# Strassen's seven products for the first matrix product of the 512-row expert tiles, and a moved half of that product

## The chip, the cores and the metric

The kernel runs on one core of a Trainium2 chip. A core has five engines that run side by side, each with its own queue of instructions taken in order: TensorE (PE, matrix products into the eight PSUM banks), VectorE (DVE), ScalarE (ACT), GpSimd (POOL, [...]which also issues the row scatters) and SyncE (SP, which issues the other DMA transfers). They wait for one another through semaphores. The metric is the device time of the one launch in microseconds (us), as the median of its timed runs.

## What is computed

The input is 8 batches of 2496 tokens of 256 channels. Each batch is filtered in the frequency domain along its tokens; then each token goes to one of 8 experts, which is a two-layer network with a ReLU between.

```python
X = np.fft.rfft(x, axis=1)
y = np.fft.irfft(X * (filt_r + 1j * filt_i)[None], n=2496, axis=1)     # (8, 2496, 256)
x = y.reshape(19968, 256)
logits = x @ w_gate                                                    # (19968, 8)
e = np.argmax(logits, axis=1)
gate = softmax(logits)[rows, e]
for each expert e, over its rows:  h = np.maximum(x[rows] @ w1[e], 0)  # w1[e]: 256 x 1024
                                   out[rows] = gate * (h @ w2[e])      # w2[e]: 1024 x 256
```

All of it is in fp32.

## The kernel before

**Transforms.** The Fourier transforms are matrix products, done batch by batch in four stages: `stage_a` (L331), `stage_b` (L344, with the filter as four VectorE instructions, L358 to L362), `stage_c` (L365) and `stage_d` (L381). Between stages the data goes to DRAM and back. The loads share a pool of input tiles (`NIN` = 8 of them, L295) and the finished rows wait in `YB` = 8 tiles until they are scattered.

**Routing.** `route` (L498) finds each token's expert on VectorE and computes a row number in a DRAM list kept by expert (`row`, L576). GpSimd scatters the rows there, one indirect DMA for each group of rows (L596). `tile_map` then cuts the lists into tiles that all hold rows of one expert: 28 tiles of 512 rows, 14 of 256 and at the end 23 of 128.

**Experts.** A tile is worked in steps. `rows_in` and `weights` issue the loads of its rows (`xg`) and of the halves of its weights: `w1t` in two halves of 512 hidden channels, `w2t` likewise, each in three buffers. `turn_x` (L716) transposes the rows on TensorE into `xT` (two blocks of 128 channels). `hidden` (L729) makes 128 hidden channels by all rows of the tile: two matmuls (L733) into one PSUM bank, and a ReLU out of it (L737) into one of nine `hT` tiles; eight such steps make the first product. `result` (L740) makes 128 output rows: eight matmuls (L747) into a bank, the gate on ScalarE or VectorE (L751, L752) into one of four `ys` tiles, and a row scatter on GpSimd (L753).

**Order.** The order on TensorE, VectorE, ScalarE and SyncE is that in which the program emits the steps. A planner (the loop from L912) does this with a clock of its own: `experts` (L875) yields expert steps with costs and with the load that each needs, the transform steps come from `STEPS`, and the planner takes an expert step when its load is due and the expert work has credit, else a transform step. Routing steps go in between. `prefetch` (L860) issues loads as buffers come free in this plan. GpSimd's order is left to the scheduler of the language. For a tile i, `experts` yields `turn_x(i)` unless it was done, eight `hidden` steps, `turn_x(i + 1)` if its rows are due, and then the `result` steps:

```python
for k in range(FT):
    yield lambda: hidden(i, k), 0.43 * n, ("w1", 2 * i + k // FH2)
...
for j in range(n):
    yield lambda: result(i, j), 3.42, ("w2", 2 * i + 1)
```

The transforms end at some 1033 us; from there on only expert tiles are left, first ten of 512 rows.

Of the kernel before, what the change touches and what calls it, by code (L numbers as in the profile page):

```python
# [22 lines left out]
E = 8  # L23
# [95 lines left out]
def kernel(  # L119
# [77 lines left out]
    tau_i = cst.tile([1, 64], I32, name="tau_i")  # L197
# [3 lines left out]
    pro = first.enter_context(tc.tile_pool(name="pro", bufs=2, side="right"))  # L201
    pools = {}
# [92 lines left out]
    NIN, YB = 8, 8  # L295
# [48 lines left out]
    def stage_b(b, f):  # L344
# [10 lines left out]
        yw = sb.tile([P, 2, D], F32, tag="yw", name="yw")  # L355
# [258 lines left out]
    def tile_map(b, rows, n, last):  # L614
# [21 lines left out]
        tau = pools["moe"].tile([1, n], F32, tag=f"tau{n}", name="tau", bufs=1)  # L636
        past = pools["moe"].tile([1, n, E - 1], F32, tag=f"past{n}", name="past", bufs=1)
# [5 lines left out]
        ef = pools["moe"].tile([1, n], F32, tag=f"ef{n}", name="ef", bufs=1)  # L643
# [5 lines left out]
        rf = pools["moe"].tile([1, n], F32, tag=f"rf{n}", name="rf", bufs=1)  # L649
# [24 lines left out]
    work, idt, gts, xgs, xts, w1t, w2t, hs = [], {}, {}, {}, {}, {}, {}, {}  # L674
# [22 lines left out]
    def weights(h, second):  # L697
# [10 lines left out]
        if second:  # L708
            w2t[h] = pools["moe"].tile([P, FH2, D], F32, tag="w2t", name="w2t", bufs=3)
            nc.sync.dma_start(out=w2t[h], in_=moe_w2[bass.ds(ev, 1), k].rearrange("o p i d -> p (o i) d"))  # L710
        else:
            pool, bufs = (late["w1"], 8) if i >= SHORT else (pools["moe"], 3)
            w1t[h] = pool.tile([P, DH, F // 2], F32, tag="w1t", name="w1t", bufs=bufs)
            nc.sync.dma_start(out=w1t[h], in_=moe_w1[bass.ds(ev, 1), k].rearrange("o p i f -> p (o i) f"))

    def turn_x(i):  # L716
# [5 lines left out]
        xts[i] = pools["moe"].tile([P, DH, 4 * P], F32, tag="xT", name="xT", bufs=1)  # L722
        for dh in range(DH):
# [3 lines left out]
            evac(xts[i][:, dh, :n * P].rearrange("p (j q) -> p j q", j=n), pt[:, :n], n * P)  # L727

    def hidden(i, k):  # L729
        m = work[i][0] * P  # L730
        p = bank()
        for dh in range(DH):
            mm(p[:, :m], lhsT=w1t[2 * i + k // FH2][:, dh, k % FH2 * P:(k % FH2 + 1) * P], rhs=xts[i][:, dh, :m],  # L733
               start=(dh == 0), stop=(dh == DH - 1))
        hT = pools["moe"].tile([P, 512], F32, tag="hT", name="hT", bufs=9)
        either(m, lambda: nc.vector.tensor_scalar_max(hT[:, :m], p[:, :m], 0.0),
               lambda: nc.scalar.activation(hT[:, :m], p[:, :m], AF.Relu))  # L737
        hs.setdefault(i, []).append(hT)

    def result(i, j):  # L740
# [4 lines left out]
        for k in range(FT):  # L745
            w2 = late["w2s"][:, bass.ds(ev, 1), k, :] if i >= SHORT else w2t[2 * i + k // FH2][:, k % FH2, :]
            mm(p[:, :D], lhsT=hs[i][k][:, j * P:(j + 1) * P], rhs=w2, start=(k == 0), stop=(k == FT - 1))  # L747
        ys = pools["moe"].tile([P, D], F32, tag="ys", name="ys", bufs=4)
# [111 lines left out]
    def prefetch():  # L860
# [6 lines left out]
        for what in ("w1", "w2"):  # L867
            h = got[what]
            if h < 2 * len(work) and rows_at[work[h // 2][3]] <= now[0] and (
                    h - used[what] < (3 if h < 2 * SHORT else 8)):  # L870
# [4 lines left out]
    def experts():  # L875

        for i in range(NT):
            n = TILES[i][0]
            if used["x"] == i:
                yield lambda: turn_x(i), 0.22 * n, ("x", i)  # L880
                used["x"] += 1
            for k in range(FT):
                yield lambda: hidden(i, k), 0.43 * n, ("w1", 2 * i + k // FH2)
                if (k + 1) % FH2 == 0:
                    w1t.pop(used["w1"])
                    used["w1"] += 1
            xts.pop(i)
            if i + 1 < NT and when.get(("x", i + 1), now[0] + 1.0) <= now[0]:
                yield lambda: turn_x(i + 1), 0.22 * TILES[i + 1][0], ("x", i + 1)
                used["x"] += 1  # L890
            for j in range(n):
# [4 lines left out]
    def share():  # L896

        known = sum(7.1 * t[0] for t in work[used["w2"] // 2:])
# [71 lines left out]
```

## Time and profile before

| | |
|---|---|
| timed runs | 1622.03 us median of 3 (1621.72 to 1622.7) |
| profiled execution, span | 1618.2 us, mean granted TensorE clock 0.989 |
| TensorE, first product of the 512-row tiles (L733) | 896 records of 128x512 |
| TensorE, second product with `w2t` (L747) | 2240 records of 128x256, 502.1 us |
| VectorE, ScalarE, GpSimd busy in 1033 to 1331 us (512-row tiles alone) | 18.59, 73.31, 47.00 us of 298 |
| data moved | 287.36 MB, 178 GB/s in the mean |

The profile is of one execution. Busy time is the time in which an engine had an instruction at work. The chain is followed back from the last instruction, at each step to what released it or to the instruction before it on its engine. A wait is put down to the instruction that ended last before it. A group is written as line, engine, operation, output tile <- input tiles, shapes and count, then busy us and mean ns of one, and then the idle time of the engine before these instructions and what ended it. An fp32 matmul appears as two records, an fp32 transpose as one.

### The profile page before, as it was taken

To read this page: it belongs to the slowest core of one execution; us is meant where nothing else is said; L and a number is where in the kernel's file an instruction comes from. 1 tells how busy PE (TensorE), PEld (TensorE's weight loads), DVE (VectorE), ACT (ScalarE), POOL (GpSimd) and SP (SyncE) were. 2 spreads that over 40 slices of the span, in tenths; PEclk is the share of its full clock that TensorE was granted. 3 is DMA by queue.
4 is the path that set the end of the run, shared out by engine and by line. 5 is a ranking of instruction groups with operands and counts; after the bars stand their busy time and mean duration, and the time that the engine had idled before them with its cause. 6 is when DMAs were issued, how large, how long until landed. Compare 5 with 4: busy or idle time off the path is not lost.

```text
span 1618.2 us, 21005 instructions
## 1 busy us (share of the span) xinstructions
PE 1567.2 (97%) x6760; PEld 1080.1 (67%) x6760; DVE 423.3 (26%) x1418; ACT 518.1 (32%) x1149; POOL 366.6 (23%) x379
## 2 busy tenths in 40 slices
PE   7989899999999999999999899999999999999998
PEld 6534456677566666666666567667676678899997
DVE  4576561624512422235222212300000000000000
ACT  4434343333322232323233232222222222333433
POOL 4132222304213221023113205411111111111111
PEclk9998999999999999999999999999999999999999
DMA  8669797887945584347434624433344446566551
GB/s 241 173 174 285 231 317 241 248 264 234 293 130 163 171 253 133 118 149 199 136 107 129 181 82 157 153 105 110 133 148 154 135 150 227 178 219 183 172 181 47
DMA packets 119265, 287.36 MB, mean 178 GB/s; under 512 B 17587, under 2 KB 58812, under 8 KB 119157
## 3 DMA queue, kind: packets, MB, share of 16 engines
q1 hardware_dynamic: 99941, 242.69, 49.8%
q0 software_dynamic: 19216, 43.33, 7.7%
q8 instruction: 55, 0.90, 0.2%
q14 instruction: 53, 0.43, 0.1%
HBM read 205.95 MB, written 80.90 MB: 177 GB/s over the span
## 4 chain that ended last, share of the span: by engine, by line
PE 89%; DMA 4%; DVE 3%; issue 2%; SPq 0%; ACT 0%; POOL 0%; POOLq 0%; ACTq 0%; DVEq 0%
PE bank L747 34%; PE bank L733 34%; PE bank L391 4%; PE bank L351 3%; PE bank L372 3%; PE bank L337 3%; PE bank L726 2%; PE bank L466 2%; DMA fin<-ud 1%; PE lt L480 1%; DMA ud<-uo 1%; DMA fin<-in_x_dram 1%; PE bank L413 1%; DMA zd<-zo 1%; DVE yw L360 1%
## 5 line engine op out<-in xcount | busy, mean ns | idle before, releaser
L733 PE MATMUL bank<-xT,w1t 128*128 128x512 f32 (+2 forms) x2080 | 589.2, 435 | 0.2 <-ACT xT L227 0.2
L747 PE MATMUL bank<-w2t,hT 128*128 128x256 f32 x2240 | 502.1, 381 | 0.3 <-issue 0.3
L733 PEld LDWEIGHTS bank<-xT,w1t 128*128 128x128 f32 x2080 | 337.7, 191 | 218.5 <-issue 196.4
L747 PEld LDWEIGHTS bank<-w2t,hT 128*128 128x128 f32 x2240 | 422.9, 191 | 74.9 <-issue 18.4
L753 POOL DMA_INDIRECT out_dram<-ys,idt x163 | 160.1, 982 | 914.3 <-ACT ys L752 604.9
L737 ACT ACTIVATE hT<-bank 128x512 f32<-128x512 f32 (+2 forms) x520 | 227.4, 438 | 360.2 <-PE bank L733 325.0
L596 POOL DMA_INDIRECT rows<-yo,row x176 | 174.8, 993 | 299.1 <-DVE gts L721 69.0
L752 ACT ACTIVATE ys<-bank,gts 128x256 f32<-128x256 f32 x157 | 74.2, 474 | 493.4 <-PE bank L747 450.6
L227 DVE COPY xT<-bank 128x128 f32<-128x128 f32 (+2 forms) x53 | 25.1, 473 | 583.3 <-PE bank L726 467.8
L372 PE MATMUL bank<-ys,tcs 128*128 128x512 f32 x140 | 74.3, 613 | 13.6 <-DVE ys L362 10.2
L358 DVE TENSOR_TENSOR ys<-bank,ht 128x512 f32<-128x512 f32 x80 | 55.1, 689 | 122.5 <-PE bank L351 83.9
L747 PE MATMUL bank<-w2s,hT 128*128 x368 | 83.2, 379 | 0.0
L391 PE MATMUL bank<-fin,tds 120*117 120x512 f32 x140 | 69.8, 622 | 12.1 <-DMA fin<-ud 12.1
L337 PE MATMUL bank<-fin,tas 117*120 117x512 f32 x154 | 73.9, 598 | 0.0
L747 PEld LDWEIGHTS bank<-w2s,hT 128*128 128x128 f32 x368 | 68.1, 190 | 8.3
L351 PE MATMUL bank<-fin,tbs 128*128 128x512 f32 x140 | 72.4, 600 | 0.0
L227 ACT COPY uo<-bank 128x512 f32<-128x512 f32 x70 | 41.0, 586 | 70.1 <-PE bank L372 51.9
L359 DVE SCALAR_TENSOR_TENSOR yw<-bank,ht 64x512 f32<-64x512 f32 x80 | 55.4, 693 | 2.6 <-POOL ht L253 1.2
L360 DVE TENSOR_TENSOR yw<-bank,ht 64x512 f32<-64x512 f32 x80 | 54.7, 684 | 1.1
L391 PEld LDWEIGHTS bank<-fin,tds 120*117 120x117 f32 x140 | 25.8, 188 | 43.4 <-issue 31.6
L227 ACT COPY yo<-bank 117x512 f32<-117x512 f32 x70 | 40.6, 589 | 41.3 <-PE bank L391 34.8
L372 PEld LDWEIGHTS bank<-ys,tcs 128*128 128x128 f32 x140 | 25.9, 193 | 39.5 <-issue 28.8
(129 smaller groups left out, 885.0 us busy)
## 6 DMA issues: line engine op xcount, KB each, us to landing
w1t<-in_moe_w_dram SPq DMA_DIRECT2D x130, 512.0 KB
w2t<-in_moe_w_dram SPq DMA_DIRECT2D x84, 512.0 KB
fin<-in_x_dram SPq DMA_DIRECT2D x40, 512.0 KB
fin<-zd SPq DMA_DIRECT2D x70, 256.0 KB
ud<-uo SPq DMA_DIRECT2D x70, 256.0 KB
zd<-zo SPq DMA_DIRECT2D x35, 480.0 KB
fin<-ud SPq DMA_DIRECT2D x35, 480.0 KB
xg<-rows SPq DMA_DIRECT2D x28, 544.0 KB
```

The costliest lines, as they stand in the source:

```text
L227: either(n, lambda: nc.vector.tensor_copy(o, i), lambda: nc.scalar.copy(out=o, in_=i))
L337: mm(p[:TK, :], lhsT=tas, rhs=xt[:TP, j:j + 2, :], start=True, stop=True)
L351: mm(p, lhsT=tbs, rhs=zi[:, j:j + 2, :], start=True, stop=True)
L360: nc.vector.tensor_mul(yw[HP:], z2[:HP], fi)
L372: mm(p, lhsT=tcs, rhs=ys, start=True, stop=True)
L391: mm(p[:TP, :], lhsT=tds, rhs=ui[:TK, j:j + 2, :], start=True, stop=True)
L596: sc = nc.gpsimd.indirect_dma_start(out=rowsd, out_offset=bass.IndirectOffsetOnAxis(ap=at, axis=0), in_=what, in_offset=None,)
L733: mm(p[:, :m], lhsT=w1t[2 * i + k // FH2][:, dh, k % FH2 * P:(k % FH2 + 1) * P], rhs=xts[i][:, dh, :m], start=(dh == 0), stop=(dh == DH - 1))
L737: lambda: nc.scalar.activation(hT[:, :m], p[:, :m], AF.Relu))
L747: mm(p[:, :D], lhsT=hs[i][k][:, j * P:(j + 1) * P], rhs=w2, start=(k == 0), stop=(k == FT - 1))
L752: lambda: nc.scalar.activation(ys, p[:, :D], AF.Copy, scale=gate))
L753: nc.gpsimd.indirect_dma_start(out=out, out_offset=bass.IndirectOffsetOnAxis(ap=idt[i].bitcast(U32)[:, j, :], axis=0), in_=ys, in_offset=None,
```

## The change

The first product of a 512-row tile is done by Strassen's method, in the form with fifteen additions. For each half of the hidden channels the weights `w1t` are seen as 2x2 blocks (128 input channels x 256 hidden channels) and the tile as 2x2 blocks (128 channels x 256 rows). Seven products of blocks (`product`, two matmuls of 256 columns each into one bank) take the place of eight. The weight sums (`w1_sums`, four additions for a half) and the row sums (four additions for a tile, at the end of `turn_x`) are made on GpSimd. The products are put together by seven VectorE additions out of PSUM and one ScalarE copy, through a tile `part` and in `hT`; two ReLUs of 1024 columns on ScalarE then work in place. Tiles of 256 and 128 rows keep the plain product.

`experts` now yields the first product by halves, and puts the first half of the next tile's first product ahead of a tile's `result` steps when its rows and weights are due by the plan. The weight sums of the next half are issued in the middle of a half, when its weights are due.

To make room, `NIN` goes from 8 to 7, `YB` from 8 to 6, `w2t` from three buffers to two, `ys` from four to three, the routing scratch tiles share buffers and two small tiles move to other pools; `xT` goes from one buffer to two, and `hT` is three tiles of half a product each. The host lays `w1` out so that a half holds two blocks of 256 channels; a load has the size it had.

```diff
-    NIN, YB = 8, 8
+    NIN, YB = 7, 6
...
-        yw = sb.tile([P, 2, D], F32, tag="yw", name="yw")
+        yw = (pro if b == 0 else sb).tile([P, 2, D], F32, tag="yw", name="yw", bufs=2 if b == 0 else 1)
...
-            w2t[h] = pools["moe"].tile([P, FH2, D], F32, tag="w2t", name="w2t", bufs=3)
+            w2t[h] = pools["moe"].tile([P, FH2, D], F32, tag="w2t", name="w2t", bufs=2)
...
-        xts[i] = pools["moe"].tile([P, DH, 4 * P], F32, tag="xT", name="xT", bufs=1)
+        xts[i] = pools["moe"].tile([P, DH, 4 * P], F32, tag="xT", name="xT", bufs=2)
...
+        if n == 4:
+            b = xts[i].rearrange("p h (r c) -> p h r c", r=2)
+            t = sums[i] = pools["moe"].tile([P, 4, 2 * P], F32, tag="sums", name="sums", bufs=2)
+            nc.gpsimd.tensor_tensor(t[:, 0], b[:, 0, 1], b[:, 0, 0], op=ALU.subtract)
+            nc.gpsimd.tensor_tensor(t[:, 1], b[:, 1, 1], t[:, 0], op=ALU.subtract)
+            nc.gpsimd.tensor_tensor(t[:, 2], b[:, 1, 1], b[:, 0, 1], op=ALU.subtract)
+            nc.gpsimd.tensor_tensor(t[:, 3], b[:, 1, 0], t[:, 1], op=ALU.subtract)
+            free["p"] = max(free["p"], now[0]) + 3.0
+
+    def w1_sums(h):
+        w = w1t[h]
+        t = wsum[h] = pools["moe"].tile([P, 4, 2 * P], F32, tag="wsum", name="wsum", bufs=2)
+        nc.gpsimd.tensor_tensor(t[:, 0], w[:, 0, 1], w[:, 1, 1], op=ALU.add)
+        nc.gpsimd.tensor_tensor(t[:, 1], t[:, 0], w[:, 0, 0], op=ALU.subtract)
+        nc.gpsimd.tensor_tensor(t[:, 2], w[:, 0, 0], w[:, 0, 1], op=ALU.subtract)
+        nc.gpsimd.tensor_tensor(t[:, 3], w[:, 1, 0], t[:, 1], op=ALU.subtract)
+        free["p"] = max(free["p"], now[0]) + 3.0
+
+    def hidden_by_quarters(h):
...
+        def product(left, right):
+            q = bank().rearrange("p (v c) -> p v c", v=2)
+            for v in range(2):
+                mm(q[:, v], lhsT=left[:, v * P:(v + 1) * P], rhs=right, start=True, stop=True)
+            return q
...
+        low = hT[:, 1, :, 0]
+        q = product(w[:, 0, 0], b[:, 0, 0])
+        nc.scalar.copy(out=part, in_=q)
+        q = product(w[:, 1, 0], b[:, 1, 0])
+        add(hT[:, 0, :, 0], q, part)
+        yield 1.71
+        q = product(ws[:, 1], t[:, 1])
+        add(part, q, part)
+        q = product(ws[:, 2], t[:, 2])
+        add(low, q, part)
+        yield 1.71
+        q = product(ws[:, 0], t[:, 0])
+        add(hT[:, 1, :, 1], q, low)
+        add(part, q, part)
+        q = product(w[:, 1, 1], t[:, 3])
+        add(low, q, low)
+        relu(hT[:, 1], hT[:, 1])
+        yield 1.71
+        q = product(ws[:, 3], b[:, 1, 1])
+        add(hT[:, 0, :, 1], q, part)
+        relu(hT[:, 0], hT[:, 0])
+        yield 0.85
...
-        ys = pools["moe"].tile([P, D], F32, tag="ys", name="ys", bufs=4)
+        ys = pools["moe"].tile([P, D], F32, tag="ys", name="ys", bufs=3)
...
+        def half(h):
+            i, g = divmod(h, 2)
+            n = TILES[i][0]
+            if n == 4:
+                if h not in wsum:
+                    yield lambda: w1_sums(h), 0.0, ("w1", h)
+                steps = hidden_by_quarters(h)
+                for m, t in enumerate((1.71, 1.71, 1.71, 0.85)):
+                    yield lambda: next(steps), t, ("w1", h)
+                    if m == 1 and due("w1", h + 1) and TILES[(h + 1) // 2][0] == 4:
+                        w1_sums(h + 1)
+                wsum.pop(h)
+            else:
+                for a in range(4):
+                    yield lambda: hidden(i, g, a), 0.43 * n, ("w1", h)
...
         for i in range(NT):
-            n = TILES[i][0]
-            if used["x"] == i:
-                yield lambda: turn_x(i), 0.22 * n, ("x", i)
-                used["x"] += 1
-            for k in range(FT):
-                yield lambda: hidden(i, k), 0.43 * n, ("w1", 2 * i + k // FH2)
...
-            if i + 1 < NT and when.get(("x", i + 1), now[0] + 1.0) <= now[0]:
-                yield lambda: turn_x(i + 1), 0.22 * TILES[i + 1][0], ("x", i + 1)
-                used["x"] += 1
-            for j in range(n):
+            yield from turned(i)
+            if used["w1"] == 2 * i:
+                yield from half(2 * i)
+            if due("x", i + 1):
+                yield from turned(i + 1)
+            yield from half(2 * i + 1)
+            if used["x"] == i + 2 and due("w1", 2 * i + 2):
+                yield from half(2 * i + 2)
+            for j in range(TILES[i][0]):
                 yield lambda: result(i, j), 3.42, ("w2", 2 * i + 1)
...
-        known = sum(7.1 * t[0] for t in work[used["w2"] // 2:])
+        known = sum(26.8 if t[0] == 4 else 7.1 * t[0] for t in work[used["w2"] // 2:])
```

## The prediction

> **What bounds the kernel now.** I read the page's busy times first, then the chain that ended last, then the granted clock and the busy times by stretch, then the groups by shape for prices.
>
> ```profile
> PE 1567.2 (97%) x6760; PEld 1080.1 (67%) x6760; DVE 423.3 (26%) x1418; ACT 518.1 (32%) x1149; POOL 366.6 (23%) x379
> PE 89%; DMA 4%; DVE 3%; issue 2%; SPq 0%; ACT 0%; POOL 0%; POOLq 0%; ACTq 0%; DVEq 0%
> ```
>
> The second line is the chain by engine. TensorE is busy 97% of the span and carries 89% of the chain, so work taken from TensorE shortens the kernel, as long as nothing makes it wait. The same chain in order of time gives its prices, undisturbed, after the transforms have ended:
>
> ```profile
> 1161.72 13.73 PE bank L733 x32
> 1176.33 13.82 PE bank L747 x64
> ...
> 1331.82 6.91 PE bank L733 x32
> ```
>
> Columns: start, length, line, count. A matrix product in fp32 shows as two records. A 512-row tile's first product (L733) takes 13.73 us in 32 records of 512 columns, 0.429 us each. The 256-row tile after 1331 takes 6.91 us in 32 records of 256 columns, 0.216 us each, and changes its PSUM bank every four records, exactly as the new products do: narrower instructions cost the same per column.
>
> ```profile
> 130.00:165.00 35.00, 30.21 (x100) 14.04 (x98) 21.52 (x74) 16.15 (x33) 5.82 (x6) 0.90 0.99 287
> 1100.00:1200.00 100.00, 100.00 (x359) 65.86 (x358) 2.52 (x9) 25.36 (x46) 13.68 (x14) 1.00 0.39 132
> ```
>
> These are stretches: busy TensorE, weight loads, VectorE, ScalarE, GpSimd, then granted clock, DMA share, GB/s. Until about 240 us there is little expert work to fill with, the DMA engines are nearly full (0.99) and TensorE has gaps; later it has none. So a step may use any other engine late, but early there is no slack.
>
> ```profile
> L358 DVE TENSOR_TENSOR ys<-bank,ht 128x512 f32<-128x512 f32 x80 | 55.1, 689 | 122.5 <-PE bank L351 83.9 <-PE bank L747 11.4 <-issue 9.5
> L737 ACT ACTIVATE hT<-bank 128x512 f32<-128x512 f32 x224 | 133.8, 598 | 274.3 <-PE bank L733 247.7 <-issue 26.5
> L362 POOL TENSOR_TENSOR ys<-ys,yw 128x512 f32<-128x512 f32 x10 | 12.7, 1268 | 15.7 <-DVE yw L360 7.7 <-PE bank L351 3.3 <-PE bank L337 3.1
> L253 POOL TENSOR_TENSOR ht<-ht,sgs 64x1024 f32<-64x1024 f32 x4 | 7.6, 1892 | 15.0 <-DMA ht<-in_filt_dram 14.8
> L253 POOL TENSOR_TENSOR ht<-ht,sgs 64x512 f32<-64x512 f32 x2 | 2.1, 1035 | 0.1
> ```
>
> Prices: an add of a PSUM bank and an SBUF tile on VectorE is 0.69 us (L358 has these operands), a 512-wide ReLU on ScalarE 0.60 us. The 224 ReLUs are eight for each of 28 tiles of 512 rows. GpSimd adds are shown at 512 and 1024 elements only.
>
> **What the Trainium skill says.** "GPSIMD Engine Reference", section 3.1, measures an add of 2048 fp32 at 4497 ns. With the 1268 ns here at 512 this gives 2.1 ns an element and, as an estimate, 0.73 us at the 256 of the change; L253's two rows give 1.67 ns an element and 0.61 us. "SBUF — State Buffer", section "Who interferes with whom", says that a VectorE instruction with at most one SBUF input does not contend with GpSimd. All seven new VectorE adds have one input in PSUM, so I add nothing for contention; no run here shows it. "ScalarE: Activation LUTs", section "What ACT_TABLE_LOAD costs", gives 186 ns + 0.833 ns an element, 1.04 us for the new 1024-wide ReLU; at 512 it gives 0.61, and the trace 0.60.
>
> **The change, part by part.** *Products.* Half a tile's first product is four steps of two 512-column matmuls now, 6.87 us. It becomes seven products of two 256-column matmuls, 28 records x 0.216 = 6.05 us. 56 halves x 0.82 = **45.9 us** off TensorE. The built program has 784 such matmuls (56 x 14), so it does what it says.
>
> *Evacuation.* Per half, VectorE gets seven adds, 7 x 0.69 = 4.83 us, and ScalarE one copy and two ReLUs, 0.59 + 2 x 1.04 = 2.67 us in place of 4 x 0.60 = 2.40. Both are below TensorE's 6.05, so the seven banks hold; a half ends some 2 us after its last matmul (add 0.69, ReLU 1.04). Nothing waits for that: the next tile's half, 6.05 us, stands in between. This is what the moved step is worth, and I put both at 0. In the transform stage VectorE's adds come on top of 20 to 37% busy (400 to 1000 us) and make it about 50 to 70% with 9.7 us a tile; the transform's own additions (L358 to L362, 2.8 us in a row) may hold an add up, so 0 to 14 us (0.8 us for each of some 18 tiles); I take 0.
>
> *GpSimd sums.* Twelve adds a tile, 12 x 0.73 = 8.8 us, and four row writes at 1.29 us from start to start, 5.2 us: 14 us of a 27 us tile. In the late stage the order on TensorE is turn, half, half of the next tile, four results. The sums needed by the third product of the next tile's half (six adds deep) start about 2.2 us after the results end and are done at 2.2 + 4.4 = 6.6; they are needed at 0.9 + 6.05 + 1.73 = 8.7. So there is 2 us to spare, and the cost is 0.
>
> *The first 512-row tile* is different. In the program's order on GpSimd its sums stand around the row scatters of the second batch: sums, one scatter, one weight sum, three sums, three weight sums, seven scatters, four weight sums. The trace of before shows when that scatter can go:
>
> ```profile
> 241.00 1.04 PE L726 MATMUL bank<-ident,xg 128*128 128x128 f32 x8
> 241.65 1.07 ACT L227 COPY xT<-bank 128x512 f32<-128x512 f32 x2 [0.36 <-PE bank L726]
> 246.19 0.17 DVE L576 CAST row<-rowf 117x8 uint32<-117x8 f32 x1
> 246.66 1.00 POOL L596 DMA_INDIRECT rows<-yo,row  x1 [20.48 <-DVE gts L721]
> 247.96 0.99 POOL L596 DMA_INDIRECT rows<-yo,row  x1 [0.30 <-issue]
> ```
>
> GpSimd waits until 246.66 for the row numbers. The sum that the third product needs is the fifth add behind that scatter: 247.96 + 5 x 0.73 = 251.6. TensorE is ready at 242.29 + 1.73 = 244.0 and waits 7.6. Then it has five products (4.3), transposes (0.5) and two products (1.7) until 258.1, while GpSimd does two adds (253.1), seven scatters (9.0, 262.1) and three adds: 264.3. It waits 6.2. TensorE takes its instructions in order, so the transforms behind it wait as well. In sum **+13.7 us**; bounds 0 (if scatters and sums fell otherwise) and 20 (adds at 1.27 us). After these gaps the clock will dip, as in the stretch 130 to 165 (0.90): +1, between 0 and 3.
>
> *The end of the transforms.* The last batch has fourteen scatters in a row (18 us) besides the 14 us of that tile, against 27: some 5 us over, less the slack. I take **+2**, between 0 and 7.
>
> *Buffers.* One input tile fewer (`NIN` 7), `YB` 6: the queue order of SyncE has some loads one or two places later, behind stores that wait for ScalarE. Where DMA was the chain before 240 us this may cost a load's latency (about 5 us) or nothing; other places gain, since nearby products are reordered. **+2**, between -3 and +8. `w2t` with two buffers: both halves load only after the results before; 1 MB at the 152 GB/s of a late tile is 7 us, hidden by two halves (12.1 us). `ys` with three: a row is written every 3.45 us and needed again after 10.4; hidden. The further `yield` rules, the 256- and 128-row tiles and the routing scratch change no count of instructions: 0.
>
> *Sum:* -45.9 + 13.7 + 1 + 2 + 2 = -27.2 us on the profiled span of 1618.2, hence 1591. The three timed runs stand 3.8 us above that span, and I make no claim on this difference: 1622.0 - 27.2 = **1595 us**.
>
> **Rivals.** (A) *No wait at the first tile*, because the scatters do not hold the sums as the order says: only -45.9 and small terms, 1576 to 1584. For it: elsewhere the sums have 2 us or more to spare. Against: GpSimd takes its queue in order, and the trace shows it idle 20 us for that scatter. Chance 0.17. (B) *Small waits in each transform-stage tile*, VectorE's adds behind the transform's own: 18 x 0.8 = 14 us more, 1604 to 1618. For it: chains of four VectorE instructions before 240 us already set the end. Against: half of VectorE is still free. Chance 0.20. (C) *GpSimd becomes the bound:* the place is the third product of each moved half, the price six adds. It decides from (8.7 - 2.2) / 6 = 1.08 us an add; at 1.5 us each of 27 tiles waits 2.5 us, 68 us, with 20 at the first tile: 1622 - 46 + 68 + 20 + 5 = 1669, slower than before. For it: the trace shows no add of this size. Against: twice the width took 1.27. Chance 0.05. That losses just eat the gain: 0.03.
>
> **Numbers.** My own case, 1585 to 1603, gets 0.55. The range for 8 in 10 reaches into A and B, 1579 to 1611. A difference under 0.2%, 3.2 us, cannot be told from none here. Faster by more: 0.92; within: 0.03; slower: 0.05.
>
> **What would show it.** The new product's line at 12.1 us for 28 pairs of a tile, and a late tile of 26.8 us where it was 28.4; TensorE waiting for GpSimd twice, 6 to 8 us each, between 240 and 270 us, and hardly elsewhere; VectorE near 690 us busy, GpSimd near 610. I am wrong if TensorE waits for GpSimd or VectorE in every tile, or if the stage before 240 us lasts over 8 us longer.

## The result, and the profile after

The change makes the kernel faster, by a quarter of what was forecast.

| | before | after |
|---|---|---|
| time, median | 1622.28 us (4 runs) | 1615.65 us (4 runs, 1614.27 to 1618.16) |
| ratio, 95% interval | | 0.9961 [0.9944, 0.9978] |
| span of the profiled execution | 1618.2 us | 1612.5 us |

The forecast was 1595 us with a range from 1579 to 1611. The time lies above that range; the sign was right.

The page of the changed kernel, its busy times and its chain by engine:

```profile
PE 1536.1 (95%) x7432; PEld 1211.1 (75%) x7432; DVE 694.7 (43%) x1797; ACT 533.5 (33%) x1106; POOL 608.5 (38%) x715
PE 31%; issue 1%; DMA 0%; POOL 0%; POOLq 0%; ACT 0%
```

VectorE (694.7) and GpSimd (608.5) are busy for what was forecast (690 and 610). TensorE's busy time fell by 31.1 us, not by 45.9, and the chain, which TensorE carried to 89% before, can be followed on it for 31% only. Its first and some later pieces, in order of time (start, length, what, count):

```profile
1090.71 0.98 DMA out_dram<-ys,idt
1091.69 4.05 issue
...
1095.91 0.98 POOL out_dram L827
...
1096.91 0.75 POOL sums L733
...
1097.73 0.73 POOL sums L734
...
1119.18 12.09 PE bank L765 x56
1131.27 13.86 PE bank L821 x64
1145.13 0.87 PE bank L727 x8
1146.00 12.09 PE bank L765 x56
```

It begins with a row write of the results, waits 4 us, goes over the next row write and two sums on GpSimd, and only then runs on TensorE; I come back to that. From there on a tile's first product takes 12.09 us in 56 records, and one tile follows the next after 26.8 us, where it was 28.4. There the change brings all it can, and TensorE waits for nothing.

The loss is in two other stretches. Busy times by stretch of the changed kernel (columns as in the prediction: stretch, length, TensorE, weight loads, VectorE, ScalarE, GpSimd, then granted clock, DMA share, GB/s):

```profile
130.00:165.00 35.00, 29.11 (x104) 14.53 (x105) 20.09 (x70) 16.30 (x33) 5.84 (x6) 0.92 1.05 324
225.00:275.00 50.00, 38.85 (x156) 28.49 (x155) 27.36 (x99) 15.35 (x30) 16.29 (x20) 0.83 0.73 238
1000.00:1110.00 110.00, 97.78 (x448) 83.78 (x447) 48.99 (x134) 28.41 (x43) 65.68 (x80) 0.95 0.38 123
1100.00:1200.00 100.00, 100.00 (x477) 88.04 (x476) 46.55 (x121) 27.41 (x41) 46.14 (x60) 0.99 0.36 116
```

and the two stretches in the kernel before:

```profile
225.00:275.00 50.00, 47.10 (x202) 28.55 (x201) 18.36 (x85) 18.26 (x37) 11.87 (x12) 1.00 0.84 279
1000.00:1110.00 110.00, 109.65 (x410) 74.47 (x409) 17.55 (x104) 26.94 (x50) 34.38 (x36) 1.00 0.41 136
```

The reader is to see two things in each pair: TensorE is idle for 8 and 12 us more, and its granted clock is lower (0.83 and 0.95 for 1.00). The second is a loss that busy time hides, since a slow matmul counts as busy.

To have both in one number I took, in each trace, the time from the start of every TensorE record to the start of the next, less the median of that time for the records of its line and shape (those that signal a semaphore are counted apart from those that don't). The medians add up to the work at full speed, the rest is what was lost to waits and to half clock.

```
                          work    lost, us, in the stretch
                        (medians)  0-225  225-275  275-1000  1000-1110  1110-end   sum
kernel before            1523.5     49.7      4.9      28.1        0.8      -0.2   83.3
changed kernel           1477.3     47.0     19.8      40.1       17.1      -0.2  123.8
difference                -46.2     -2.7    +14.9     +12.0      +16.3       0.0  +40.5
```

-46.2 + 40.5 = -5.7 us is the difference of the two spans. So the products bring what was forecast, and 40 us of waits and half clock take most of it away: 15 at the first 512-row tile, 16 at the end of the transforms, 12 spread between them, less 3 ahead of them.

*The first 512-row tile*, TensorE in the changed kernel (start, length, line, what it does, count, and the wait before it):

```profile
238.62 0.66 PE L537 MATMUL rk<-oe,tri 117*117 117x64 f32 x2 [3.44 <-DVE oe L526]
...
241.23 3.66 PE L765 MATMUL bank<-xT,w1t 128*128 128x256 f32 x8
249.55 5.48 PE L765 MATMUL bank<-sums,wsum 128*128 128x256 f32 x12 [4.66 <-POOL wsum L744]
...
257.03 1.89 PE L765 MATMUL bank<-xT,w1t 128*128 128x256 f32 x8
261.98 4.39 PE L765 MATMUL bank<-sums,wsum 128*128 128x256 f32 x12 [3.06 <-POOL wsum L744]
...
267.94 1.24 PE L806 MATMUL bank<-xT,w1t 128*128 128x256 f32 x5
```

Eight records take 1.89 us at full clock (257.03) and 3.66 at half (241.23). The tile takes 267.94 - 241.23 = 26.7 us, where its products and transposes need 12.6. Of the 14.1 us lost, 7.7 are the two waits for GpSimd that the prediction named, and the other 6.4 are nearly all half clock (5.9 by the trace's record of the clock). Not all of it follows from these two waits: the first eight records are slow already. Ahead of them TensorE had waited 3.44 us for the routing (L537). In the kernel before that wait is 2.66 us long, and no half clock follows it.

*The end of the transforms.* GpSimd first, then ScalarE, then TensorE:

```profile
1080.31 0.73 POOL L746 TENSOR_TENSOR wsum<-w1t,wsum 128x256 f32<-128x256 f32 x1
1081.21 1.00 POOL L827 DMA_INDIRECT out_dram<-ys,idt  x1 [0.17 <-issue]
1087.53 0.99 POOL L827 DMA_INDIRECT out_dram<-ys,idt  x1 [5.32 <-ACT ys L826]
1090.71 0.98 POOL L827 DMA_INDIRECT out_dram<-ys,idt  x1 [2.20 <-issue]
1095.91 0.98 POOL L827 DMA_INDIRECT out_dram<-ys,idt  x1 [4.22 <-ACT part L778]
1096.91 0.74 POOL L733 TENSOR_TENSOR sums<-xT 128x256 f32<-128x256 f32 x1
```

```profile
1086.87 0.47 ACT L826 ACTIVATE ys<-bank,gts 128x256 f32<-128x256 f32 x1 [11.92 <-DMA out_dram<-ys,idt]
```

```profile
1087.39 2.07 PE L765 MATMUL bank<-sums,wsum 128*128 128x256 f32 x4 [5.82 <-ACT ys L826]
...
1098.51 4.26 PE L765 MATMUL bank<-sums,wsum 128*128 128x256 f32 x12 [4.69 <-POOL sums L734]
```

From 1058 to 1081 us GpSimd works without a pause on fourteen row scatters and eight weight sums. The four row writes of the results (L827) come behind them. ScalarE, with three result buffers, waits 11.9 us for the first of them to land before it can write the fourth result, and behind it in its queue stands the evacuation of TensorE's banks: TensorE waits 5.8 us. The sums of the next tile stand behind the four row writes: TensorE waits another 4.7. What is odd is how the row writes go: not one every 1.29 us as the scatters do, but over 14.7 us.

### The profile page after: what moved, and what is told of

It reads as the page before. It is cut to its first block, busy times and chain, and to the rows that moved or that the text cites. A ratio compares the mean times of both kernels' runs of the same rounds, so it can differ in the third digit from the quotient of the medians.

```text
span 1612.5 us, 23212 instructions
## 1 busy us (share of the span) xinstructions
PE 1536.1 (95%) x7432; PEld 1211.1 (75%) x7432; DVE 694.7 (43%) x1797; ACT 533.5 (33%) x1106; POOL 608.5 (38%) x715
## 5 line engine op out<-in xcount | busy, mean ns | idle before, releaser
L827 POOL DMA_INDIRECT out_dram<-ys,idt x163 | 160.8, 986 | 610.8 <-ACT ys L826 326.4
L596 POOL DMA_INDIRECT rows<-yo,row x176 | 175.0, 994 | 223.1 <-issue 54.5
L773 ACT ACTIVATE hT<-hT 128x1024 f32<-128x1024 f32 x112 | 113.7, 1052 | 292.9 <-DVE hT L769 253.2
L806 PE MATMUL bank<-xT,w1t 128*128 128x128 f32 (+1 forms) x1184 | 191.9, 317 | 0.3 <-issue 0.3
L765 PE MATMUL bank<-sums,wsum 128*128 128x256 f32 x672 | 165.9, 393 | 19.4 <-POOL wsum L744 7.7
L806 PEld LDWEIGHTS bank<-xT,w1t 128*128 128x128 f32 x1184 | 169.3, 193 | 20.0 <-issue 9.3
L765 PEld LDWEIGHTS bank<-sums,wsum 128*128 128x128 f32 x672 | 129.7, 197 | 50.4 <-issue 10.5
L769 DVE TENSOR_TENSOR hT<-bank,part 128x512 f32<-128x512 f32 x168 | 115.6, 688 | 117.5 <-ACT part L778 63.0
L812 ACT ACTIVATE hT<-bank 128x128 f32<-128x128 f32 (+1 forms) x295 | 93.4, 318 | 81.7 <-PE bank L806 68.2
L765 PE MATMUL bank<-xT,w1t 128*128 128x256 f32 x448 | 108.5, 386 | 0.4 <-ACT yo L227 0.4
L765 PEld LDWEIGHTS bank<-xT,w1t 128*128 128x128 f32 x448 | 83.7, 193 | 15.3 <-issue 3.3
L769 DVE TENSOR_TENSOR part<-bank,part 128x512 f32<-128x512 f32 x112 | 76.7, 685 | 18.0 <-PE bank L765 14.5
L769 DVE TENSOR_TENSOR hT<-bank,hT 128x512 f32<-128x512 f32 x112 | 76.8, 685 | 8.9 <-PE bank L765 4.2
L391 PE MATMUL bank<-fin,tds 120*117 120x512 f32 x140 | 69.6, 620 | 7.4 <-DMA fin<-ud 7.4
```

What stands on the lines that cost most here:

```text
L391: mm(p[:TP, :], lhsT=tds, rhs=ui[:TK, j:j + 2, :], start=True, stop=True)
L596: sc = nc.gpsimd.indirect_dma_start(out=rowsd, out_offset=bass.IndirectOffsetOnAxis(ap=at, axis=0), in_=what, in_offset=None,)
L765: mm(q[:, v], lhsT=left[:, v * P:(v + 1) * P], rhs=right, start=True, stop=True)
L769: nc.vector.tensor_tensor(o, q, a, op=ALU.add)
L773: nc.scalar.activation(o, q, AF.Relu)
L806: mm(p[:, :m], lhsT=w1t[2 * i + g][:, dh, fh, v * P:(v + 1) * P], rhs=xts[i][:, dh, :m], start=(dh == 0), stop=(dh == DH - 1))
```

## The experiments

Each ratio is against the kernel before, timed in the same set on the same chip. Ratios of different sets compare badly: the changed kernel as it is gave 0.9961 in the first set and 0.9916 in another. So what one edit does is read from the stretch that it concerns, in its trace. "Lost" is the number defined above.

### The parts of the change one by one

**Plain products, moved half kept.** `STR` is the set of tiles that use the seven products; here it is empty.

```diff
-        if n == 4:
+        if i in STR:
...
-            if n == 4:
+            if i in STR:
                 if h not in wsum:
```

> The changed kernel with the seven products taken out again: all 512-row tiles use the plain first product (32 records of 512 columns), but the moved half and the smaller buffers stay. No GpSimd sums, no VectorE adds. My theory (the order and the buffers cost and bring nothing by themselves; what was lost was lost by the sums and adds of the seven products): 1618 to 1626 us, the time of the kernel before, no TensorE wait over 3 us at 240 to 270 us and at 1075 to 1100 us. Rival (the reordering and the smaller buffers themselves cost what is missing): 1632 us or more, with the waits at 1075 to 1100 us still there.

Measured: 1631.12 us, ratio 1.005 [1.003, 1.0069]. Lost: 8.2 us from 225 to 275 and 3.9 from 1000 to 1110, where the changed kernel has 19.8 and 17.1. So most of those two losses belongs to the seven products. But the time lies between the two forecasts, 5 us above the upper end of the forecast, 8.7 above the kernel before, and from 275 to 1000 it loses 36.5, nearly as much as the changed kernel (40.1), without one of its VectorE adds.

**Neither seven products nor the moved half**: the edit above, and

```diff
-            if used["x"] == i + 2 and due("w1", 2 * i + 2):
-                yield from half(2 * i + 2)
```

> Only the smaller buffers (seven input tiles, six of the routed rows, two of the second weights, three of the result rows, one hidden tile of half a tile's width) and the halves' grain, with plain products and without the moved half. My theory: 1619 to 1626 us, the time of the kernel before, because no buffer ran out there without GpSimd's new work. Rival (the smaller buffers alone make the loss at the end of the transforms): 1630 us or more, with ScalarE waiting for row writes at 1075 to 1100 us.

Measured: 1623.58 us, 1.0001 [0.9987, 1.0015]. The smaller buffers, together with the halves' grain, cost nothing that can be told.

**Seven products without the moved half**, the last edit alone.

> The changed kernel without the moved half: a tile's second product stands directly behind both halves of its own first product. My theory: the results' third step (hT of the second half) waits for the last add (0.69 us) and the last ReLU (1.05 us) with 0.86 us of matmuls to hide behind, about 1.1 us in each of 28 tiles, 31 us in all, with some clock dips on top: 1640 to 1660 us; a late tile 27.9 to 28.8 us where it is 26.8. Rival (the move is worth nothing, because transform steps or ScalarE's lead hide the end of a half): within 4 us of the changed kernel, 1612 to 1620 us.

Measured: 1694.41 us, 1.0447 [1.0427, 1.0468], worse than either theory. A late tile:

```profile
1217.04 1.03 PE L821 MATMUL bank<-w2t,hT 128*128 128x256 f32 x4
1219.88 13.22 PE L821 MATMUL bank<-w2t,hT 128*128 128x256 f32 x60 [1.81 <-ACT hT L773]
```

After four records the second product waits 1.81 us for the last ReLU. The tile lasts 28.9 us. TensorE waits for L773 26 times, 65.8 us in all, and by the trace's record of the clock TensorE is at half speed for 98 us of the span, where it was 61 in the changed kernel. More is lost from 275 to 1000 us (84.4, where the changed kernel loses 40.1) than after 1110 (35.1, where it loses nothing). In this late tile a half ends 0.86 + 1.81 = 2.7 us after its last matmul, not 2; in the changed kernel the move is what hides it.

### The end of the transforms

**Five result buffers.** The room is that of `part`.

```diff
-        part = pools["moe"].tile([P, 2, 2 * P], F32, tag="part", name="part", bufs=1)
+        part = hT[:, 0, :, 1]
...
-        add(hT[:, 0, :, 1], q, part)
+        add(part, q, part)
...
-        ys = pools["moe"].tile([P, D], F32, tag="ys", name="ys", bufs=3)
+        ys = pools["moe"].tile([P, D], F32, tag="ys", name="ys", bufs=5)
```

> The changed kernel with five buffers for the result rows in place of three; the 2 KB come from `part`, whose partial sums now lie in the quarter of the hidden tile that they end in. My theory: ScalarE's 11.9 us wait for a row write near 1075 us goes, and with it TensorE's 5.8 us and the half clock after it, 7 to 9 us; the sums of the next tile still stand behind four delayed row writes on GpSimd, so a wait of 4 to 5 us near 1086 us stays: 1606 to 1610 us. Rival 1 (GpSimd's backlog, not the buffers, sets that stretch): the wait only moves to GpSimd's sums, 1613 to 1617 us. Rival 2 (both waits were the buffers'): 1600 to 1603 us.

Measured: 1611.74 us, 0.9937 [0.9914, 0.9959]. GpSimd and TensorE in this run:

```profile
1077.03 1.00 POOL L827 DMA_INDIRECT out_dram<-ys,idt  x1 [0.17 <-issue]
1083.96 0.98 POOL L827 DMA_INDIRECT out_dram<-ys,idt  x1 [5.93 <-ACT hT L778]
1087.15 0.98 POOL L827 DMA_INDIRECT out_dram<-ys,idt  x1 [2.20 <-issue]
1090.33 0.98 POOL L827 DMA_INDIRECT out_dram<-ys,idt  x1 [2.20 <-issue]
```

```profile
1092.91 5.49 PE L765 MATMUL bank<-sums,wsum 128*128 128x256 f32 x12 [11.18 <-POOL sums L734]
```

ScalarE's wait for a row write is gone, and TensorE waits 11.2 us for the sums instead. From 1000 to 1110 us 17.5 are lost, as before the edit (17.1). The time lies between the ranges of my theory and of the first rival; the trace has what the rival named, the wait moved to the sums. So the buffers alone were not the cause. The lines show the next one. All four results had been ready since 1075 us, and still the row writes start 6.9, 3.2 and 3.2 us apart, with GpSimd idle between them. The program gives the reason: each row write waits until the one before has landed, since both write the output; the scatters of the routing are declared to write rows of their own and don't wait. The same wait is in the kernel before. There a result comes every 3.45 us, so a spacing of 3.2 limits nothing.

**Row writes that don't wait for each other.** The rows of two tiles are never the same, so nothing is needed in the wait's place.

```diff
+        tc.declare_no_dep(sc.ins, group="results", reason="rows of their own")
+        tc.add_to_no_dep_group("results", sc.ins)
```

> The changed kernel, with the row writes of the results (L827) declared to write rows of their own, so that none of them waits until the one before has landed; three result buffers as before. My theory, new after the runs so far (near 1080 us GpSimd is held up by row writes that wait for each other, 3.2 us from start to start and once 6.9, where the scatters go every 1.29): the sums of the next tile come early and TensorE's 4.7 us wait for them goes, with some half clock; ScalarE still waits for its result buffer and TensorE 5 to 6 us with it: 6 to 8 us less than the changed kernel, 1608 to 1611 us. Rival (the burst of fourteen scatters alone makes GpSimd late): within 3 us of the changed kernel, 1613 to 1618 us.

Measured: 1609.20 us, 0.9932 [0.9909, 0.9956]. The wait for the sums is gone and 4.8 us of wait for ScalarE's result stay, as forecast; lost from 1000 to 1110: 9.0.

**Both edits.**

> Row writes that don't wait for each other, and five result buffers (`part` in the hidden tile). My theory (the loss at the end of the transforms needs both causes, row writes in single file and three buffers): four row writes at 1.29 us and two sums behind the burst end about 2 us after TensorE is ready; the 15.8 us lost between 1050 and 1110 us shrink to 2 to 5: 1601 to 1606 us, and no ScalarE wait for a row write. Rival (the burst alone): TensorE still waits 8 us or more for a sum near 1085 us, 1609 us or more.

Measured: 1600.28 us, 0.9876 [0.985, 0.9902].

```profile
1079.68 1.00 POOL L827 DMA_INDIRECT out_dram<-ys,idt  x1 [0.17 <-issue]
1080.98 0.99 POOL L827 DMA_INDIRECT out_dram<-ys,idt  x1 [0.30 <-issue]
1082.27 0.98 POOL L827 DMA_INDIRECT out_dram<-ys,idt  x1 [0.30 <-issue]
1083.55 0.98 POOL L827 DMA_INDIRECT out_dram<-ys,idt  x1 [0.30 <-issue]
```

```profile
1086.14 2.86 PE L765 MATMUL bank<-sums,wsum 128*128 128x256 f32 x12 [1.76 <-POOL sums L734]
```

The four row writes now go at 1.29 us, and TensorE waits 1.8. Lost from 1000 to 1110: 4.6. Within this set the five buffers bring 0.6% once the row writes are free (0.9932 to 0.9876), while alone they brought nothing in that stretch. Two causes stand one behind the other there.

**The kernel before with free row writes**, the same two lines at L753.

> The kernel before, with its row writes (L753) freed from waiting for each other and nothing else. My theory (the wait between row writes is there in both kernels, but shows only where GpSimd falls behind, which the sums and adds made it do): no difference, 0.998 to 1.002. Rival (it cost the kernel before too): 0.996 or less.

Measured: 1612.77 us, 0.9994 [0.9984, 1.0004]. No difference: the wait is old, and it costs something only in the changed kernel, where GpSimd has more to do.

### The first 512-row tile

```diff
+    STR = {i for i in range(NT) if TILES[i][0] == 4 and (i != FIRST4)}
```

> The changed kernel with the plain product for the first 512-row tile alone (no sums for it on GpSimd). My theory (that tile's sums stand behind row scatters; 7.7 us of waits and about 6 us of half clock): 13 us come back and 1.6 us of the products' gain is given up: 1603 to 1606 us; 250 to 275 us at 24 us busy or more. Rival (the row scatters and routing of the second batch would make that stretch as slow without the sums): 1613 to 1617 us.

Measured: 1603.31 us, 0.9887 [0.9863, 0.9911]. Lost from 225 to 275: 6.6 us, of which 3.7 are a wait for the routing (L537), where the changed kernel loses 19.8. The theory holds: with this tile's sums 13 us of that stretch's loss go, their waits and the half clock with them. The end of the transforms, untouched, loses 14.0.

### The stretch between

**The routing's counting product later.**

```diff
-        for _ in range(10):
+        for _ in range(16):
             yield
```

> The changed kernel with the counting product of the routing (L537) put sixteen places after the step before it, where it was ten. My theory (VectorE's new adds make the routing's chain late, so that TensorE meets L537 too early: 7.4 us in three waits where the kernel before had 2.7 in one): the waits at L537 go and 4 to 6 us come back with the clock: 1609 to 1612 us. Rival (the place isn't the cause, the wait comes later at the logits, the row scatters or the loads): 1614 to 1618 us.

Measured: 1609.71 us, 0.9931 [0.991, 0.9952]. The time is in the forecast, the reason is not:

```profile
PE bank L765 <- POOL sums L734: 13.5, 4, 5.5
...
PE rk L537 <- DVE oe L526: 5.7, 1, 5.7
```

(line, what it waited for, us in all, times, longest.) One wait of 5.7 us at L537 has come in place of three with 7.4, and from 275 to 1000 the loss is the same, 41.1. What time this run has gained lies ahead of 225 us (39.5 lost, 47.0 before the edit). The theory isn't shown, and the gain itself is not sure, as the changed kernel without this edit gave 0.9916 in another set.

**Plain products with the kernel's old buffers**, with the moved half and without it. The rule that loads the second weights follows their third buffer; the lines are left out here.

```diff
-    NIN, YB = 7, 6
+    NIN, YB = 8, 8
...
-        ys = pools["moe"].tile([P, D], F32, tag="ys", name="ys", bufs=3)
+        ys = pools["moe"].tile([P, D], F32, tag="ys", name="ys", bufs=4)
...
-            w2t[h] = pools["moe"].tile([P, FH2, D], F32, tag="w2t", name="w2t", bufs=2)
+            w2t[h] = pools["moe"].tile([P, FH2, D], F32, tag="w2t", name="w2t", bufs=3)
```

> Plain products for all tiles and the moved half, with the buffers of the kernel before (eight input tiles, eight of the routed rows, three of the second weights, four result rows). If the smaller buffers made the loss of the run with plain products and moved half (1.005 of the kernel before): 0.998 to 1.002. If the moved half itself made it, by using up the expert work that fills TensorE's waits at other places: 1.004 to 1.008 again, with 10 us more lost between 275 and 1050 us than in the kernel before (28.9). My guess is the moved half.

> The same without the moved half: apart from the halves' grain and the place of the transposes (ahead of a tile's second half) it is the kernel before. Either theory: 0.998 to 1.002. If it is 1.004 or more, the grain or the place of the transposes is a cause that I have not thought of.

Measured: 1619.76 us, 1.0041 [1.0025, 1.0056], with the move; 1608.83 us, 0.9975 [0.9964, 0.9987], without it, which is a little better than I had forecast. With these buffers the move costs 10.9 us, with the smaller ones it cost 7.5 (1631.12 against 1623.58), so the buffers are not the cause of that loss, the moved half is. Against the run with the smaller buffers and no move (1.0001), this one without the move is 0.26% better, some 4 us: that much the buffers may cost, as far as two sets can be compared. In the two traces here 34.0 and 23.0 us are lost from 275 to 1000 us; in the pair with smaller buffers it is 36.5 and 33.0, so one pair of traces does not place the cost firmly. The wait that differs most between 275 and 1050 us, with the move and then without it:

```profile
PE bank L391 <- DMA fin<-ud: 13.3, 2, 7.3
```

```profile
PE bank L391 <- DMA fin<-ud: 3.8, 2, 2.8
```

Here the transforms read back what they have just stored, and expert work has to fill the time. That the moved half has used up this filler is what I take from it; it was not tried by itself. With the smaller buffers the same wait is 11.1 and 4.7 us from 275 to 1000. But in the changed kernel it is 5.2 us there, and 8.4 in the kernel before.

### Without the move, and all together

**The end of a half hidden in another way**: no moved half; the second product takes the slices of the last ReLU last; the next tile's transposes stand behind the second half.

```diff
-        for k in range(FT):
+        for at, k in enumerate((0, 1, 4, 5, 6, 7, 2, 3)):
...
-            if due("x", i + 1):
-                yield from turned(i + 1)
             yield from half(2 * i + 1)
-            if used["x"] == i + 2 and due("w1", 2 * i + 2):
-                yield from half(2 * i + 2)
+            if due("x", i + 1):
+                yield from turned(i + 1)
```

> Seven products without the moved half, but the second product takes the hidden slices in the order 0, 1, 4, 5, 6, 7, 2, 3 (the ones of the last ReLU last, 2.6 us of matmuls ahead of them), and the next tile's transposes stand behind the second half (0.9 us more). My theory: the wait of 1.8 us in each tile goes, late tiles last 26.8 us again, and what the move cost in the transform stage, 8 to 11 us, comes back too: 0.985 to 0.991 of the kernel before, faster than the changed kernel. Rival (VectorE's seven adds, not the last ReLU, end a half late, and only another half's work can cover it): still 1 us or more at each tile, 1.01 or more.

Measured: 1638.15 us, 1.0115 [1.0095, 1.0134]. Late tiles run at 26.8 us without the move, as I expected, but from 275 to 1000 us 54.4 are lost, 14 more than in the changed kernel. The longest waits from 275 to 1050 us:

```profile
PE bank L372 <- DVE ys L362: 8.9, 3, 5.5
PE rk L537 <- DVE oe L526: 5.9, 3, 3.2
PE bank L727 <- DVE part L769: 4.2, 1, 4.2
```

These are waits for VectorE, whose queue holds the seven adds among the transforms' own instructions. They are not mainly waits for the end of a half: the second product waits for its ReLU (L773) for 3.2 us in all there. My theory was wrong for that stage. The ratio is where the rival had it, but its wait of 1 us or more in each late tile isn't there. Why VectorE is later without the move, no run shows.

**The three mendings** (free row writes, five result buffers, plain first tile) with the move, with the later counting product, and without the move (there with the order of slices and the place of the transposes of the run above):

> The changed kernel with row writes that don't wait for each other, five result buffers and the plain product for the first 512-row tile. My theory (the two stretches at 240 to 275 and 1050 to 1110 us are separate losses, 13 and 14 us): the gains add, 0.979 to 0.983 of the kernel before, some 1586 to 1593 us, with 12 us or so still lost between 275 and 1050. Rival (one stretch only hides the other, or the schedule moves a loss elsewhere): 0.985 or more.

> The same, and the routing's counting product sixteen places later. If that place is a cause of its own (theory of the run that moved it alone): another 4 to 5 us less, 0.976 to 0.980 of the kernel before. If its gain alone came by chance from where other waits fell, as its trace suggests (5.7 us at L537 stayed): within 3 us of the version with three, either way.

> The changed kernel once more, as it is, so that the versions of this set stand beside it on the same chip: 0.994 to 0.998 of the kernel before, by every theory.

> The same with the three mendings (row writes that don't wait for each other, five result buffers, plain product for the first 512-row tile). If the move is what keeps costing between 275 and 1050 us: 5 to 10 us less than the version with the move and the mendings, 0.977 to 0.982 of the kernel before. Rival (the sums of the next tile come too late without the move, behind the row writes): slower than that version.

> The version with the moved half and the three mendings, beside the two on the same chip: 0.982 to 0.986 of the kernel before, by either theory.

| version | set | us | ratio |
|---|---|---|---|
| changed kernel as it is | A | 1600.47 | 0.9916 [0.989, 0.9942] |
| three mendings | A | 1587.77 | 0.9838 [0.9818, 0.9857] |
| and the later counting product | A | 1586.88 | 0.9831 [0.9812, 0.9849] |
| three mendings, again | B | 1609.82 | 0.9941 [0.9924, 0.9959] |
| three mendings, without the move | B | 1629.20 | 1.0063 [1.0047, 1.008] |

In set A the mended version is 12.7 us faster than the changed kernel and 25.6 faster than the kernel before (1613.34 there), at the edge of the forecast; the changed kernel itself did better than forecast. The later counting product adds nothing that can be told: its trace loses 17.3 us from 225 to 275, where the three mendings lose 4.2, now to waits for a load of rows (4.4 us) and for the routing (3.9), and 8.7 less from 275 to 1000. So in this schedule one small loss can take the place of another. Without the move the mended version is slower than the kernel before and loses 61.1 us from 275 to 1000, where it loses 49.2 with the move in the same set: the theory that the move only costs between 275 and 1000 us fell a second time. Set B has no run of the changed kernel; there the same mended program gains 10.2 us only, less than forecast, and its trace loses 49.2 from 275 to 1000 us (36.9 in A) and 13.4 from 1000 to 1110 (7.9 in A). Why is open. A piece of the end of the transforms is left in A too: with the first tile plain, the scatters fall otherwise, and TensorE still meets sums that stand among them:

```profile
1042.35 4.27 PE L768 MATMUL bank<-sums,wsum 128*128 128x256 f32 x12 [4.67 <-POOL sums L737]
```

## Why the prediction was wrong

**Products, -45.9: right.** 12.09 us a tile, a late tile of 26.8, and 46.2 us less work.

**GpSimd sums late, 0, and evacuation, 0: right after 1110 us, with the move in place.** Nothing is lost there; the rows of the page have the prices:

```profile
L773 ACT ACTIVATE hT<-hT 128x1024 f32<-128x1024 f32 x112 | 113.7, 1052 | 292.9 <-DVE hT L769 253.2
...
L765 PE MATMUL bank<-sums,wsum 128*128 128x256 f32 x672 | 165.9, 393 | 19.4 <-POOL wsum L744 7.7
...
L769 DVE TENSOR_TENSOR hT<-bank,part 128x512 f32<-128x512 f32 x168 | 115.6, 688 | 117.5 <-ACT part L778 63.0
...
L743 POOL TENSOR_TENSOR wsum<-w1t 128x256 f32<-128x256 f32 x56 | 41.8, 747 | 106.4 <-PE bank L765 99.2
```

Add on VectorE 688 ns (0.69 was taken), ReLU of 1024 on ScalarE 1052 ns (1.04 was the estimate), add on GpSimd 747 ns. The estimate of 0.73 us from the Trainium skill's "GPSIMD Engine Reference", section 3.1, holds, and rival C with it fell.

**The first tile, +13.7: right in sum by luck, wrong in its parts.** The stretch loses 14.9 us more. The waits are 4.7 and 3.1 us, not 7.6 and 6.2: the first scatter went at 245.02 where I had it at 246.66, and the second half's waits shrank with the first half's slower products. Half clock made up for it: by the record of the clock it costs 7.2 us from 225 to 275 (half of TensorE's busy time in it), and nothing in the kernel before.

**The clock, +1: mis-sized.** It is those 7.2 us, of which 3.0 follow the wait for the routing, a wait that the prediction did not have; at the end of the transforms another 3.3 come, where it had none. The Trainium skill says in "TensorE: Matmul & The Clock Gate", section "What's actually happening", that after an idle window of about 3.4 us the clock falls to half, and that it takes a busy window to come back. This trace agrees: 8 records take 3.66 us for 1.89 and 12 take 5.48 for 2.75 behind waits of 3.4 and 4.7 us, and the three dips last 6.83, 6.83 and 3.41 us. I had forecast two waits above that length and priced the clock at less than one window. The half clock after a wait does not grow with the wait. Over the 19 traces of this case, after their first 20 us, TensorE waits 3 us or more 111 times; half clock followed each time and cost 2.2 us in the mean, 3.2 at most, and as much for waits of 3 to 4 us as for those of 6 and more (2.2 and 2.4). It followed 41 of the 58 waits of 2.0 to 2.9 us as well, though shorter gaps close by may have their part in that.

**The end of the transforms, +2: the step that failed.** It was "fourteen scatters in a row (18 us) besides the 14 us of that tile, against 27: some 5 us over, less the slack". The lost time is 16.3 us, and the 14.3 above the forecast are two thirds of the whole miss of 21.5. Its term for "four row writes at 1.29 us from start to start, 5.2 us" was taken from the scatters (L596), which don't wait for each other; the row writes do, and took 14.7 us from the first start to the last, 3.2 to 6.3 each (6.9 in the run with five buffers). With them free and enough result buffers they go at 1.29 and the stretch loses 4.6. The step "`ys` with three: a row is written every 3.45 us and needed again after 10.4; hidden" failed for the same reason: it holds only while GpSimd is not behind. Neither alone explains the loss: five buffers alone leave 17.5 us in that stretch, free row writes alone 9.0, both 4.6.

**Buffers, +2: right for the buffers (1.0001 and, across sets, some 4 us), and short of the move.** "This is what the moved step is worth, and I put both at 0" looked at what the move hides, not at what it takes. With plain products it costs 7.5 and 10.9 us (1.005 against 1.0001, 1.0041 against 0.9975). For the seven products it is a bargain all the same: 79 us are lost without it as the program stands (1694.41 against 1615.65, across sets).

**Rivals.** The time fell where (B) had it, 1604 to 1618 us, for the most part for another reason: the first tile and the end of the transforms lose 31.2 of the 40.5 us. Small waits for VectorE are there: from 275 to 1000 us TensorE waits 4.0 us for the routing (L537) and 3.3 for the new adds (L769), and in the kernel before for neither in that stretch. That is about half of (B)'s 14. (A) fell with the first tile's waits.

**The sum again**, each stretch with its measured loss: -46.2 + 14.9 + 16.3 + 12.0 - 2.7 = -5.7 us, where the prediction had -45.9 + 13.7 + 1 + 2 + 2 = -27.2. The cause of the 12.0 stays open. The move has a cost with plain products, but the wait that grew with it there (L391) is not longer in the changed kernel than before; the waits for VectorE are. And the number is not firm: the changed kernel's other profiled execution loses 29.9 us in that stretch, 10 less, and waits there for these two lines 4.7 us in place of 7.3. That fits its better ratio in that set, but no run shows what makes the difference.

## What to carry to other kernels

Before work is added to a queue that runs in order, take the spacing of what stands behind it as it is when it is queued: an operation that always came at leisure hides its own wait, and a look-alike row that doesn't wait is the wrong price. To a TensorE wait of three microseconds or more, add some two for the half clock that follows it, whatever its length: several waits of three cost more than one long one of the same sum. And a step moved to hide one end can cost elsewhere; a run with the move alone, without the work that it is for, tells that price.

## What the runs showed that I had not expected

- Row writes to one tensor that wait for each other's landing go 3.2 us apart (1.29 without the wait), and the first two of them 6.3 to 6.9 us apart behind fourteen scatters.
- The half clock after a TensorE wait of 3 us or more costs 2.2 us in the mean, and no more after one of 11.2 us (3.1 in the run with five buffers) than after one of 3.44 (3.0).
- The end of a half can be hidden by the order of the next product's slices alone in the late stage (26.8 us a tile without the move); while transforms share VectorE, that version loses 14 us more than the changed kernel.
- One and the same program stood at 0.9838 of the kernel before in one set and at 0.9941 in another. An effect of a few microseconds in this kernel has to be looked for in its own stretch of the trace.
